# Letting the first three loads of w2 wait only for the last readers of their buffers

## The chip, the cores and the metric

One NeuronCore of a Trainium2 chip. The time is the device time of one execution in microseconds (us). Every run also records the span from first to last instruction and the mean granted TensorE clock (1.0 is full speed). A run is labelled slow because it is over 1.5% above the fastest of its kernel, and is left out of the comparison.

Names in the profiles: PE is the matrix engine and PEld its loads of weights, DVE the vector engine, ACT the scalar engine, and SPq the queue of the SP engine, which issues the transfers (DMA). In this program the matmuls read their operands from SBUF (`arena` in the profiles) and add up their products in banks of PSUM (`ps`).

A ratio is the mean time of one kernel's fast runs over the mean of the other's in the same rounds, so it is not quite the ratio of the medians that are quoted. Ratios carry a 95% interval.

## The reference, cut to what matters

```python
def reference(A_x, A_wqkv, A_wo, B_x, B_w1, B_b1, B_w2, B_b2, gate_w):
    x = A_x                                            # (1, 2048, 512) bf16
    g = sigmoid((x * gate_w).sum(-1, keepdims=True))
    a = local_attention(x, A_wqkv) @ A_wo              # 32 heads, window 8, dilation 2
    h = layernorm(x)                                   # the MLP is called with x as well
    u = gelu(einsum("bsd,sf->bdf", h, w1) + b1)        # w1: 2048 x 1792
    b = (einsum("bdf,fs->bds", u, w2) + b2).transpose(0, 2, 1)   # w2: 1792 x 2048
    return g * a + (1 - g) * b
```

(Condensed.) The end of the kernel computes 16 output tiles of 128 rows. Each is 14 matmuls with w2 (the second product of the MLP) and 4 with wo (the projection of the attention output), accumulated in one PSUM bank. w2 comes in as eight blocks of 256 columns (896 KB); one block serves two output tiles.

## The kernel before

The kernel lists its operations with resource names that they read and write. A small scheduler of its own orders them on each engine, then turns dependences into semaphore waits. A later writer of a name depends on the last writer and on all readers since.

```python
    def add(self, eng, fn, dur, reads=(), writes=(), deps=(), after=(), prio=0, name="", delay=0.0):
        ...
        for d in deps:
            if d is not None:
                op.deps.add(d)          # a wait
        for d in after:
            if d is not None:
                op.order.add(d)         # order of issue only, no wait
        ...
        for w in writes:
            lw = self.last_w.get(w)
            if lw is not None:
                op.deps.add(lw)
            for rd in self.readers.get(w, ()):
                op.deps.add(rd)
            self.readers[w] = []
            self.last_w[w] = op
        ...
    def users(self, names):             # last writers and readers, without becoming a writer
        ...
```

Memory is overlaid. w2 has three block buffers: two in the space of an attention buffer called pb1, one in the space of the wqkv weights.

```python
        W2S = [view("PBUF", BF16, [(256, NFT), (1, 256)], extra=4 * S),
               view("PBUF", BF16, [(256, NFT), (1, 256)], extra=4 * S + NFT * 256),
               view("WQKV", BF16, [(256, NFT), (1, 256)])]
```

The first three loads:

```python
        def ld_w2(j2):
            ds = sch.dsem("w2_%d" % j2)
            al = []
            if j2 < 2:
                al = ["pb1"]
            elif j2 == 2:
                al = ["wqkv%d_%d" % (tn, dt) for tn in range(3) for dt in range(4)]
            return sch.dma("sp", mk_dma(W2S[j2 % 3], w2v[:, :, 256 * j2:256 * j2 + 256]), F * 256 * 2, ds,
                           writes=["w2s%d" % (j2 % 3)] + al, after=d_w1[-1:], name="d_w2_%d" % j2)
        for j2 in range(3):
            ld_w2(j2)
```

Blocks 0 and 1 both "write" pb1, though their bytes do not overlap. So block 1 depends on block 0 having landed.

The same SP queue issues 16 SBUF-to-SBUF copies of the attention weights, `er0r` (4, small) and `er1`, `er2`, `er3` (4 each, 288 KB each). The first four feed the end of the first quarter of a DVE chain (line 776), the others its second, third and fourth quarter. The projection matmuls read its outputs. The consumers at the end:

```python
        for i in range(NST):                       # 16 output tiles
            j2 = i // 2
            bank = YB[i % len(YB)]                 # 7 PSUM banks, so PE may run ahead with w2
            ...
            for half in range(2):                  # line 839 (840 after the change)
                last_main[0] = A("pe", f_ph3(i, bank, half), 1.515, reads=[... "w2s%d" % (j2 % 3)], ...)
            if i % 2 == 1 and j2 + 3 <= 7:
                ld_w2(j2 + 3)
            A("pe", f_wo(i, bank), 0.865, reads=["ot%d" % (i // 4), "wo"], ...)   # line 848 (849)
            ...
```

## Time and profile before

| | before |
|---|---|
| time, median of the first 3 runs (these and a later one: 184.32 to 184.94) | 184.63 us |
| PE busy | 92% of the span |
| PE's longest wait | 9.7 us, for a load of w2 |
| mean granted clock | 0.972 |

The page of before: PE's busy time, then 40 slices of 4.6 us each, with PE's busy share and the granted clock in tenths.

```profile
PE 167.9 (92%) x876; PEld 79.3 (43%) x892; DVE 139.7 (76%) x118; ACT 66.3 (36%) x94; POOL 0.9 (0%) x8
...
PE   7999999999999999999999993059999999999993
...
PEclk9999999999999999999999999756999999999999
```

PE is busy but for one hole in slices 24 to 26, and the clock dips just behind it. The waits of PE in before (us in total, times, longest) name the hole:

```profile
PE ps L839 <- DMA arena<-in_B_w_dram: 9.7, 1, 9.7
```

PE's timeline of before (start, us, engine, line, operation, count, idle time before and its releaser):

```profile
105.03 6.21 PE L839 MATMUL ps<-arena 128*128 128x512 bf16 x28
120.91 16.65 PE L839 MATMUL ps<-arena 128*128 128x512 bf16 x62 [9.67 <-DMA arena<-in_B_w_dram]
```

Two output tiles (28 matmuls, block 0), then nothing until block 1 lands. The SP queue's timeline of before shows why it lands late:

```profile
84.97 5.80 SPq L439 DMA_DIRECT2D arena<-in_B_w_dram  x3
90.81 21.38 SPq L439 DMA_DIRECT2D arena<-arena  x16
112.24 24.20 SPq L439 DMA_DIRECT2D arena<-in_B_w_dram  x4
```

The three loads at 84.97 are the last block of w1, then blocks 0 and 2 of w2. The 16 copies follow, and block 1 goes out only at 112.24. The chain that ended last, in before (start, us, what):

```profile
110.65 1.55 SPq L439
...
112.24 8.62 DMA arena<-in_B_w_dram
...
120.91 6.07 PE ps L839 x14
...
127.03 10.52 PE ps L839 x48
```

The chain runs through the issue of the copies into block 1's load and then PE. The first 14 matmuls take 6.07 us, twice what 14 take elsewhere (3.02).

In this trace the granted clock changed on a grid of 3.413 us: its half-speed stretch is 10.24 us (three times 3.413), its full-speed stretches are 112.64 us (33 times) and 58.03 us (17 times). Stretches laid on that grid are called clock windows here. Columns: from:to, length, then busy time (count) of PE, PEld, DVE, ACT and POOL, then granted clock, DMA share, GB/s.

```profile
109.70:113.11 3.41, 1.54 (x8) 0.49 (x5) 3.41 (x2) 0.00 (x0) 0.00 (x0) 1.00 0.97 184
113.11:116.53 3.42, 0.00 (x0) 0.00 (x0) 3.42 (x3) 0.00 (x0) 0.00 (x0) 1.00 0.79 180
116.53:119.94 3.41, 0.00 (x0) 0.00 (x0) 3.41 (x3) 0.00 (x0) 0.00 (x0) 0.50 0.92 278
119.94:123.36 3.42, 2.45 (x6) 0.89 (x7) 3.35 (x3) 0.00 (x0) 0.00 (x0) 0.50 0.83 218
123.36:126.77 3.41, 3.41 (x9) 1.22 (x8) 3.38 (x2) 0.00 (x0) 0.00 (x0) 0.50 0.00 0
126.77:130.18 3.41, 3.36 (x16) 1.57 (x16) 3.41 (x2) 0.00 (x0) 0.00 (x0) 1.00 0.00 0
```

In this trace the window with PE busy for 45% (1.54 of 3.41) was followed by full clock (1.00), the wholly idle one after it by half clock (0.50).

### The profile page before, as it was taken

What the parts mean: (1) busy time and instruction counts of PE and PEld (TensorE: products, weight loads), DVE (VectorE), ACT (ScalarE), POOL (GpSimd) and SP (SyncE); (2) the same over time, 40 slices, a digit from 0 to 9 for tenths busy, and PEclk for the clock granted to TensorE, in tenths of its full rate; (3) what the DMA queues carried; (4) which work ended last, traced back from release to release, by engine and by line L of the source; (5) the groups of instructions that cost most, each with busy time, mean ns of one, the idle gap of its engine ahead of it and who ended that gap; (6) DMA issues with size and microseconds to landing.
All of it is one profiled execution on the core that took longest, in us unless ns stands there. A gap on an engine that the chain in (4) does not pass through costs nothing.

```text
span 183.0 us, 2127 instructions
## 1 busy us (share of the span) xinstructions
PE 167.9 (92%) x876; PEld 79.3 (43%) x892; DVE 139.7 (76%) x118; ACT 66.3 (36%) x94; POOL 0.9 (0%) x8
## 2 busy tenths in 40 slices
PE   7999999999999999999999993059999999999993
PEld 2855455454444444444444441023444444444441
DVE  0755679999799993689999999999999999800000
ACT  2476668775391115794121110000001231111165
POOL 1000000000000000000000000000000000000000
PEclk9999999999999999999999999756999999999999
DMA  5999799900000626179999899780247356300014
GB/s 184 296 234 235 178 266 314 246 0 5 0 2 5 171 59 188 45 220 243 295 290 214 205 195 185 219 228 0 79 126 228 106 152 193 94 29 31 30 65 135
DMA packets 43101, 27.42 MB, mean 150 GB/s; under 512 B 7892, under 2 KB 42324, under 8 KB 42708
## 3 DMA queue, kind: packets, MB, share of 16 engines
q1 hardware_dynamic: 43092, 27.28, 59.5%
q8 instruction: 7, 0.11, 0.2%
q14 instruction: 2, 0.02, 0.0%
HBM read 18.88 MB, written 2.10 MB: 115 GB/s over the span
## 4 chain that ended last, share of the span: by engine, by line
PE 68%; SPq 11%; DVE 7%; DMA 7%; ACT 4%; issue 1%
PE ps L839 25%; PE ps L586 19%; SPq L439 11%; PE ps L800 9%; PE ps L848 8%; DMA arena<-in_B_w_dram 5%; PE ps L668 4%; DMA arena<-in_A_wqkv_dram 2%; DVE arena L713 2%; DVE arena L776 2%; PE ps L609 2%; DVE arena L761 2%; ACT arena L727 1%; ACT L727 1%; ACT L564 1%
## 5 line engine op out<-in xcount | busy, mean ns | idle before, releaser
L776 DVE TENSOR_TENSOR arena<-arena 128x2048 bf16<-128x2048 bf16 (+2 forms) x32 | 71.5, 2287 | 0.4
L839 PE MATMUL ps<-arena 128*128 128x512 bf16 x220 | 52.8, 395 | 9.9 <-DMA arena<-in_B_w_dram 9.7
L800 PE MATMUL ps<-arena 128*128 128x512 bf16 x218 | 48.5, 379 | 0.3
L839 PEld LDWEIGHTS ps<-arena 128*128 128x128 bf16 x224 | 22.6, 101 | 38.5 <-DMA arena<-in_B_w_dram 10.2
L586 PE MATMUL ps<-arena 128*128 128x512 bf16 x171 | 38.3, 379 | 0.6 <-issue 0.2
L661 DVE TENSOR_TENSOR arena<-arena 128x8192 bf16<-128x8192 bf16 x8 | 35.0, 4421 | 1.2 <-ACT arena L597 1.2
L866 ACT ACTIVATE arena<-ps,arena 128x512 bf16<-128x512 f32 x16 | 12.4, 777 | 62.5 <-PE ps L848 62.0
L800 PEld LDWEIGHTS ps<-arena 128*128 128x128 bf16 x224 | 21.7, 98 | 26.8 <-issue 0.8
L586 PEld LDWEIGHTS ps<-arena 128*128 128x128 bf16 x176 | 19.6, 114 | 18.6 <-ACT arena L597 0.6
L597 ACT ACTIVATE arena<-ps 128x512 bf16<-128x512 f32 x32 | 19.0, 598 | 7.1 <-PE ps L586 6.9
L813 ACT ACTIVATE arena<-ps,arena 128x512 bf16<-128x512 f32 x14 | 9.6, 687 | 30.8 <-PE ps L800 30.7
L848 PE MATMUL ps<-arena 128*128 128x512 bf16 x63 | 15.4, 379 | 0.1
L551 DVE BATCH_NORM_STATS2 arena<-arena 128x6 f32<-128x512 bf16 x16 | 9.9, 680 | 6.6 <-DMA arena<-in_A_x_dram 6.6
L848 PEld LDWEIGHTS ps<-arena 128*128 128x128 bf16 x64 | 6.3, 98 | 7.5
L713 DVE TENSOR_TENSOR arena<-arena 128x256 bf16<-128x256 bf16 (+4 forms) x16 | 7.9, 506 | 2.0 <-ACT arena L727 1.7
L594 ACT ACTIVATE arena<-ps 128x512 bf16<-128x512 f32 x12 | 7.2, 596 | 3.1 <-PE ps L586 3.1
L668 PE MATMUL ps<-arena 128*32 128x512 bf16 x128 | 7.5, 380 | 0.0
L698 ACT ACTIVATE arena<-ps 128x1024 bf16<-128x1024 f32 x4 | 4.0, 1020 | 5.0 <-PE ps L638 3.8
L570 DVE TENSOR_SCALAR arena<-arena 128x512 bf16<-128x512 bf16 x16 | 5.3, 405 | 0.0
L668 PEld LDWEIGHTS ps<-arena 128*32 128x32 bf16 x128 | 3.1, 96 | 4.1 <-issue 0.4
L513 PE MATMUL ps<-arena 128*128 128x512 bf16 x9 | 3.7, 563 | 1.1 <-POOL arena L426 1.1
L609 PE MATMUL ps<-arena 128*128 128x256 bf16 x32 | 3.7, 273 | 0.2 <-DMA arena<-in_A_wqkv_dram 0.2
(50 smaller groups left out, 36.4 us busy)
## 6 DMA issues: line engine op xcount, KB each, us to landing
arena<-in_B_w_dram SPq DMA_DIRECT2D x7, 1024.0 KB, 6.4
arena<-in_B_w_dram SPq DMA_DIRECT2D x8, 896.0 KB, 7.0
arena<-arena SPq DMA_DIRECT2D x12, 288.0 KB, 5.8
arena<-in_A_x_dram SPq DMA_DIRECT2D x4, 512.0 KB, 5.1
out_dram<-arena SPq DMA_DIRECT2D x16, 128.0 KB, 1.7
arena<-in_A_wqkv_dram SPq DMA_DIRECT2D x3, 512.0 KB, 4.5
arena<-arena SPq DMA_DIRECT2D x8, 128.0 KB, 3.0
arena<-in_A_wo_dram SPq DMA_DIRECT2D x1, 512.0 KB, 8.1
```

The lines of the kernel that those rows point to most:

```text
L439: return lambda e: e.dma_start(dst, src)
L551: A("dve", (lambda t_: (lambda e: e.bn_stats(out=ST6[:, t_, :], in_=X[:, t_, :])))(t), 0.7, reads=["x%d" % t], writes=["st6_%d" % t], name ...
L586: ins = e.matmul(ps[:, bank, :], lhsT=lhsT, rhs=XT[:, sb, dt, :], start=(dt == 0), stop=(dt == 3))
L597: return lambda e: e.activation(out=dst, in_=ps[:, bank, :], func=AF.Copy)
L661: return lambda e: e.tensor_tensor(out=PBL[buf], in0=in0, in1=in1, op=ALU.mult)
L668: ins = e.matmul(ps[32 * c:32 * c + 32, 4 + wl, :], lhsT=RP, rhs=PBL[buf][:, wl, c * 512:(c + 1) * 512], start=(dl == 0), stop=(dl == 3), ...
L713: return A("dve", lambda e: e.tensor_tensor(out=o_, in0=a_, in1=b_, op=op_), dur, reads=rd, writes=wr, name=nm)
L776: A("dve", lambda e: e.tensor_tensor(out=o_, in0=a_, in1=b_, op=op_), dur, reads=rd, writes=wr, name=nm)
L800: ins = e.matmul(ps[:, bank, :], lhsT=W1W[:, slot, st, 128 * e_:128 * e_ + 128], rhs=X[:, st, :], start=(st == 0), stop=(st == NST - 1))
L839: ins = e.matmul(ps[:, bank, :], lhsT=W2S[slot][:, ft, 128 * e_:128 * e_ + 128], rhs=UT[:, ft, :], start=(ft == 0), stop=False)
L848: ins = e.matmul(ps[:, bank, :], lhsT=OT[:, t, 128 * i:128 * i + 128], rhs=WO[:, t, :], start=False, stop=(t == 3))
L866: A("act", (lambda e, i=i, bank=bank: e.activation(out=OUTS[:, i, :], in_=ps[:, bank, :], func=AF.Identity, scale=col(OMG, i), bias=col(C2 ...
```

## The change

The intent: the loads should depend only on the last users of the memory that they overwrite, and be issued in the order in which they are read.

```diff
         def ld_w2(j2):
             ds = sch.dsem("w2_%d" % j2)
-            al = []
-            if j2 < 2:
-                al = ["pb1"]
-            elif j2 == 2:
-                al = ["wqkv%d_%d" % (tn, dt) for tn in range(3) for dt in range(4)]
-            return sch.dma("sp", mk_dma(W2S[j2 % 3], w2v[:, :, 256 * j2:256 * j2 + 256]), F * 256 * 2, ds,
-                           writes=["w2s%d" % (j2 % 3)] + al, after=d_w1[-1:], name="d_w2_%d" % j2)
+            al = w2_al[0 if j2 < 2 else 1] if j2 < 3 else ()
+            op = sch.dma("sp", mk_dma(W2S[j2 % 3], w2v[:, :, 256 * j2:256 * j2 + 256]), F * 256 * 2, ds,
+                         writes=["w2s%d" % (j2 % 3)], deps=al, after=(d_w1[-1:] + d_w2[-1:]) if j2 < 3 else (), name="d_w2_%d" % j2)
+            d_w2.append(op)
+            return op
+
+        d_w2 = []
+        w2_al = [sch.users(["pb1"]), sch.users(["wqkv%d_%d" % (tn, dt) for tn in range(3) for dt in range(4)])]
         for j2 in range(3):
             ld_w2(j2)
```

In the scheduled program this swaps blocks 1 and 2 in the SP queue and drops one wait. The other engines' orders stay. The diff also adds an order of issue among the three loads (`after=`).

## The prediction

> **What bounds the kernel now.** The page gives PE 92% busy and 68% of the chain that ended last. The waits by engine show one long PE wait: the matmuls of line 839 (second MLP product, w2) wait 9.7 us for a load of w2. PE's timeline: 28 matmuls of line 839 (output tiles 0 and 1, from the first w2 buffer) end at 111.2 us, then nothing until 120.91. The clock table (windows of 2 us) shows the second cost: granted clock 1.0 until about 116.5, then 0.5 until about 126.8, so the first 14 matmuls after the hole take 6.07 us where every later batch of 14 takes 3.02.
>
> Why that load is late: it is w2 block 1. Blocks 0 and 1 name the same overlaid resource as written, so block 1 waits for block 0's completion. The scheduler therefore places it after block 2 and after the 16 SBUF-to-SBUF copies (issued 90.81 to 112.2 us). It is issued at 112.24 and lands at 120.86 (8.62 us in the chain). Blocks 0 and 2, issued before the copies, land at about 94.5 and 97.6; block 2 is not read before tile 4. By 112 the wait itself is long satisfied: what costs is the place in the SP queue.
>
> **What the change does.** The instruction orders of PE, DVE, ACT and POOL stay. On SP, blocks 1 and 2 swap places and one wait (on block 0) goes. No work is added or removed. So block 1 should land near 97.6 us, and block 2 should be issued near 112.2 and land near 120.9.
>
> **Critical path.** PE then runs tiles 2 and 3 straight on: 28 x 0.216 = 6.05 us, 111.2 to 117.2. It waits for block 2 from 117.2 to 120.9, about 3.7 us instead of 9.7. Gain for certain: 6.0 us. Second term, the clock. [...] the slow stretch is 10.24 us, three times 3.41, and starts 5.3 us after PE went idle. [...] I expect the clock mostly to stay at 1.0, which saves the other 3.0 us (6.07 less 3.02). Sum: 9.0 us with the clock kept, 6.0 if it falls. I give the kept clock about three in four.
>
> What could take it back: tile 6 needs block 3, which lands at 123.7 now and is wanted at 127. Block 4 can be issued at 117.3 instead of 130, and is wanted after 132. The DVE chain (line 776) ends at 159.5 and feeds the last group of output-projection matmuls of line 848, which start at 174.0 now and would start at 165. Each keeps several us of slack, so the gain should last to the end.
>
> **Prediction.** 175.9 us (184.63 less 9.0, plus part of the chance of a cold clock), 8 in 10 between 175.0 and 179.0. Chances: faster by over 2% 0.96, within 2% 0.03, slower 0.01.
>
> **What would show it right.** One PE wait of 3 to 4 us for a w2 load in place of 9.7; 56 matmuls of line 839 before it; a clock of 1.0 through it; the matmuls after it at 3.0 us per 14; the 16 copies and the DVE chain where they were; the last PE group near 165.
>
> **What would make it wrong.** The clock falling to 0.5 at a 3.7 us hole (result about 178.6). Block 2, now behind the copies, landing later than 121. Block 1 not landed by 111. Block 4's earlier issue slowing blocks 2 or 3. PE running into the DVE chain.

The reasons given for the second term are cut where marked, since no trace of this case shows them. 6.0 us for the hole and 3.0 us for the clock (6.07 less 3.02) make 9.0, and 6.0 if the clock falls.

## The result, and the profile after

| | before | after |
|---|---|---|
| time, median of 4 runs (range) | 184.49 (184.32 to 184.94) | 178.54 (177.09 to 178.89) |
| ratio | | 0.9659 (0.96 to 0.9718) |
| PE's wait for a w2 load | 9.7 | 3.8 |
| mean granted clock of the 4 runs | 0.972 in the profiled run | 0.990, 0.989, 0.990, 0.990 |

The page of after (slices of 4.4 us; PE is now 95% busy):

```profile
PE   7999999999999999999999999974999999999993
...
PEclk9999999999999999999999999997899999999999
```

The hole is narrower, but the clock still dips. The waits of PE in after:

```profile
PE ps L840 <- DMA arena<-in_B_w_dram: 3.8, 1, 3.8
```

PE's timeline and, in the second fence, the SP queue's timeline of after:

```profile
105.61 12.25 PE L840 MATMUL ps<-arena 128*128 128x512 bf16 x56
121.64 9.36 PE L840 MATMUL ps<-arena 128*128 128x512 bf16 x35 [3.79 <-DMA arena<-in_B_w_dram]
```

```profile
85.54 6.08 SPq L439 DMA_DIRECT2D arena<-in_B_w_dram  x3
91.66 21.46 SPq L439 DMA_DIRECT2D arena<-arena  x16
113.16 7.83 SPq L439 DMA_DIRECT2D arena<-in_B_w_dram  x3
```

Four tiles (56 matmuls) now run before the hole instead of two. The copies stand where they stood, and the load behind them is now block 2. The trace's completion events put block 1 at 98.5 us, block 2 at 121.6. The chain that ended last, in after:

```profile
113.16 8.43 DMA arena<-in_B_w_dram
...
121.64 9.36 PE ps L840 x35
131.00 0.86 PE ps L849 x4
```

The 35 matmuls behind the hole take 9.36 us; at full clock 35 take 7.73 (an experiment's trace below). The clock windows of after, laid on this trace's own grid, with the columns as before:

```profile
118.17:121.58 3.41, 0.00 (x0) 0.00 (x0) 3.39 (x3) 0.00 (x0) 0.00 (x0) 1.00 1.02 299
121.58:124.99 3.41, 3.35 (x8) 1.19 (x9) 3.32 (x3) 0.00 (x0) 0.00 (x0) 0.50 1.20 291
124.99:128.40 3.41, 3.41 (x17) 1.57 (x16) 3.41 (x1) 0.00 (x0) 0.00 (x0) 1.00 0.43 110
```

The spans differ by 6.60 us (183.0 and 176.4). The sum from the two traces: the hole, 3.79 less 9.67, gives -5.88. From the first w2 matmul to the first projection matmul, without the hole, before takes 137.56 - 105.03 - 9.67 = 22.86 and after 131.00 - 105.61 - 3.79 = 21.60: -1.26, the clock. The first w2 matmul starts 0.58 later in after, in a part that the change does not touch (PE waits 0.5 there for a load of x): +0.58. From the first projection matmul to the end, 45.44 and 45.40: -0.04.

So the hole gave what it should. The clock, expected to give 3.0, gave 1.3 in this pair of traces.

### The profile page after: what moved, and what is told of

Same layout as the page of the kernel before. It is cut to its first block, busy times and chain, and to the rows that moved or that the text cites. A ratio compares the mean times of both kernels' runs of the same rounds, so it can differ in the third digit from the quotient of the medians.

```text
span 176.4 us, 2143 instructions
## 1 busy us (share of the span) xinstructions
PE 168.1 (95%) x892; PEld 79.4 (45%) x892; DVE 139.7 (79%) x118; ACT 66.3 (38%) x94; POOL 0.9 (0%) x8
## 4 chain that ended last, share of the span: by engine, by line
PE 58%; SPq 17%; DMA 11%; DVE 8%; ACT 4%; issue 1%
PE ps L840 22%; PE ps L586 14%; SPq L439 12%; PE ps L800 10%; PE ps L849 8%; DMA arena<-in_B_w_dram 5%; SPq L460 4%; PE ps L668 4%; DMA arena<-in_A_x_dram 4%; DMA arena<-in_A_wqkv_dram 3%; DVE arena L713 3%; DVE arena L776 2%; DVE arena L761 2%; ACT arena L727 1%; ACT L727 1%
## 5 line engine op out<-in xcount | busy, mean ns | idle before, releaser
L542 DVE COPY arena<-ps 128x512 bf16<-128x512 bf16 x2 | 0.8, 425 | 4.0 <-PE ps L525 3.9
```

## The experiments

Every experiment gave a correct result. Ratios are to the kernel before, in the same rounds (its medians in the experiments: 184.6, 184.4, 184.69). "Runs with a dip" are those with a mean clock of 0.99 or less (0.989 and below included); the others have 0.997 or more.

| run | edit | median us | ratio (95% interval) | hole in its trace | runs with a dip |
|---|---|---|---|---|---|
| after (first result) | none | 178.54 | 0.9659 (0.96 to 0.9718) | 3.79 | 4 of 4 |
| e1_old_place_no_wait | blocks in the old places, no wait | 184.46 | 1.001 (0.9946 to 1.0074) | 9.93 | 4 of 4 |
| e2_new_place_wait | new places, wait kept | 179.97 | 0.9757 (0.9702 to 0.9812) | 5.95 | 4 of 4 |
| e3_after_fill16 | after, hole filled | 176.26 | 0.9561 (0.9515 to 0.9607) | 0.53 | 0 of 6 |
| e4_before_fill43 | before, hole filled | 182.18 | 0.9879 (0.9833 to 0.9926) | 0.26 | 0 of 6 |
| e5_after_fill3 | after, 3 fillers | 177.99 | 0.9647 (0.9608 to 0.9686) | 3.42 | 5 of 6 |
| e8_after_fill5 | after, 5 fillers | 177.29 | 0.9641 (0.9596 to 0.9686) | 2.74 | 5 of 6 |
| e5b_after_fill8 | after, 8 fillers | 175.52 | 0.9525 (0.949 to 0.9559) | 1.83 | 0 of 5, and the slow run |
| after_again | none | 178.18 | 0.9671 (0.9632 to 0.971) | 3.80 | 6 of 6 |
| e6_three_ahead | three blocks ahead of the copies | 173.48 | 0.9409 (0.9373 to 0.9446) | 0.86 | 0 of 4 |
| e7_third_mid | block 2 between the copies | 172.23 | 0.9347 (0.9302 to 0.9392) | none | 0 of 4 |

Four kernels move a load in the SP queue after scheduling and before waits are planned, so that dependences are kept:

```diff
         total_est = sch.schedule()
+        def mv(name, behind):
+            sp = sch.order["sp"]
+            op, prev = [[o for o in sp if o.name == n_][0] for n_ in (name, behind)]
+            sp.remove(op)
+            sp.insert(sp.index(prev) + 1, op)
+            op.start = prev.start + 1e-6
         sch.plan_waits()
```

### Is it the wait or the place in the queue? (e1, e2)

The theory was that the wait had long been satisfied when block 1's turn came, and that its effect was to make the scheduler put block 1 behind the copies. The rival was that the wait itself cost the time.

e1, on the changed kernel:

```diff
+        mv("d_w2_2", "d_w2_0")
+        mv("d_w2_1", "d_er3_3")
```

> The changed kernel with blocks 1 and 2 of w2 put back in their old places in the SP queue (block 1 behind the 16 copies), but still without the wait on block 0. Theory (the place in the queue is everything, the wait itself had long been satisfied): the same as the kernel before, 184.5 us within 0.5 %, with a hole of 9.7 us before the matmuls of the third output tile and about 10 us of clock at 0.5. Rival (the removed wait is what gains): 178.5 us, as the changed kernel.

Measured: 184.46 us, ratio 1.001. PE's timeline of e1:

```profile
121.17 15.65 PE L840 MATMUL ps<-arena 128*128 128x512 bf16 x62 [9.93 <-DMA arena<-in_B_w_dram]
```

The wait is gone, the 9.9 us hole is back, and so is the time. The wait by itself was worth nothing where it stood.

e2, the converse, on the changed kernel:

```diff
         for j2 in range(3):
             ld_w2(j2)
+        d_w2[1].deps.add(d_w2[0])
...
+        mv("d_w2_1", "d_w2_0")
```

> The changed kernel with the same order of the SP queue, but block 1 again waits for block 0 to land. Theory: block 0 lands at about 95.5 us, so the SP queue stands from about 89.5 to 95.5 and the copies behind it start near 96 instead of 91.7; they then catch up partly[...]. Block 2 lands 2 to 4 us later than 121.6, the hole grows from 3.8 to 6 to 8 us, the DVE chain starts its second quarter later; time 180.5 to 182.5. Rival (the wait costs nothing at all, wherever it stands): 178.5.

Measured: 179.97 us, a small miss: less loss than the 180.5 to 182.5 expected. The SP queue's timeline of e2:

```profile
84.82 9.90 SPq L439 DMA_DIRECT2D arena<-in_B_w_dram  x3
94.76 19.32 SPq L439 DMA_DIRECT2D arena<-arena  x16
```

The wait holds the queue (9.90 us for three loads instead of 6.08). The copies behind it catch up part of that (19.32 us instead of 21.46), all of it at the first copy (0.85 us instead of 3.10); the other fifteen take 18.43 us here and 18.32 in after. Block 1's load took the queue 2.95 us to issue in after, behind loads that had not landed, and 0.37 us in e2, where the queue had first waited for block 0 to land. That the outstanding transfers cause this was not tested. The hole grows to 5.95 us and the DVE chain waits 1.3 us for a copy. So with the old wait the new place still gives most of the gain (ratio 0.9757 against 0.9659). Dropping the wait is needed only so that the queue does not stand in the new place.

### What does the clock cost? (e3, e4)

Matmuls of no use, ones times ones into a PSUM bank that nobody reads any more, keep PE busy in the hole. On the changed kernel (e4: on the kernel before, `i == 2` and 43):

```diff
         for i in range(NST):
...
+            if i == 4:
+                last_main[0] = A("pe", f_warm_on(16, 3), 0.01, reads=["ones"], writes=["bank3"],
+                                 after=[last_main[0]], name="fill", prio=0)
             for half in range(2):
```

> The changed kernel with 16 matmuls of no use (3.46 us at full clock, into a PSUM bank that nobody reads) in the hole of 3.8 us before the fifth output tile. Theory (the matmuls behind the hole ran at half clock for one window because the hole was idle): the clock stays at 1.0 through the hole, the 35 matmuls behind it take 7.6 us instead of 9.36, and the time falls by about 1.8 us, to 176.7. Rival (the slow 35 matmuls come from something else, such as data or transfers landing): the clock still falls or the matmuls stay at 9.4 us; 178.5.

> The kernel before with 43 matmuls of no use (9.29 us at full clock) in its hole of 9.7 us. Theory: the load still lands near 120.9, the clock stays at 1.0, the 14 matmuls behind the hole take 3.0 us instead of 6.07, and the time falls by about 3.0 us, to 181.5. That is the clock's share of the hole in the kernel before. Rival: no change, 184.5.

PE's timeline behind the fillers, in e3 and then in e4:

```profile
121.10 7.73 PE L840 MATMUL ps<-arena 128*128 128x512 bf16 x34 [0.53 <-DMA arena<-in_B_w_dram]
```

```profile
120.67 13.54 PE L839 MATMUL ps<-arena 128*128 128x512 bf16 x61 [0.26 <-DMA arena<-in_B_w_dram]
```

(A matmul or two is missing from such counts in a trace.) Both expectations held, e4's with 182.18 us where 181.5 was expected. The load still lands when it did; the matmuls behind it run at full speed: 7.73 us instead of 9.36 after, 13.54 instead of 16.65 before.

The four kernels (hole as it was or shortened, clock dipping or kept) form a square. With the clock kept, shortening the hole is worth (0.9879 - 0.9561) x 184.6 = 5.9 us. The prediction had 6.0. The dip costs (1 - 0.9879) x 184.6 = 2.2 us before (interval 1.4 to 3.1; the trace says 16.65 - 13.54 = 3.1). After, it costs (0.9659 - 0.9561) x 184.6 = 1.8 us, across two calls (the trace says 9.36 - 7.73 = 1.6). So of the dip's cost the change saves 1.5 us by the traces (3.1 less 1.6) and 0.4 us by the ratios (2.2 less 1.8), whose intervals of 0.8 us and more either way are too wide to tell the two apart. It shortens the dip, but does not remove it.

### Why does the clock fall at a hole of 3.8 us? (e5, e5b, after_again, e8)

The trace of before (full clock after the window of 45%, half clock after the idle one) allows two theories. Theory A, on which the prediction counted: the clock falls only after a wholly idle window. A 3.8 us hole holds one only for (3.79 - 3.41) / 3.41 = 11% of the grid's positions, an estimate from the trace's hole and grid. Yet all four runs of after dipped, and the one traced had just that position. Theory B: a window that is mostly idle is enough. The experiments shrink the hole with fewer fillers (3, 8 or 5 in place of 16 in the diff above).

> The changed kernel with 3 matmuls of no use (0.65 us) at the start of its hole, which so shrinks from 3.8 to about 3.15 us: less than one clock window of 3.41 us, so no window can be wholly idle. Theory A (the clock falls only after a window that is wholly idle, and the changed kernel's four runs with clock 0.99 just met that phase): the mean clock is 0.998 or more in all runs and the time is about 176.7 us. Theory B (a window that is mostly idle is enough): the mean clock is 0.99 in most runs, the time 177 to 178.5.

> The same with 8 matmuls (1.73 us), which leaves a hole of about 2.1 us, at most 60 % of a window. Theory A and a theory B with its threshold above 60 % idle: clock 0.998 or more in all runs, 176.7 us. Theory B with a lower threshold: 0.99 in some runs.

> The changed kernel again, unaltered, for more runs and a second trace. Theory B, now with the threshold between 55 and 67 % idle that the traces so far allow: with a hole of 3.8 us nearly every phase of the window gives a drop, so the mean clock is 0.99 in at least five of six runs, and the time is 178.3 us within 1 us. Theory A (only a wholly idle window): 0.998 or more in most runs and about 176.7 us.

> The changed kernel with 5 matmuls of no use (1.08 us) at the start of the hole, which leaves 2.7 to 2.9 us, always shorter than a window. Theory B: a drop in roughly half to nine tenths of the runs, which shows as a mean clock of 0.99, and a bimodal time, near 178 with the drop and near 176.3 without; in the trace the window that ends with a drop is at least 55 % idle. Theory A: never a drop, 176.3 us.

Clock windows of after_again, then of e5, e8 and the end of e7 (a kernel of the next section), each on its trace's own grid and with the columns as before (PE busy follows the length, the clock is third from the end).

```profile
116.64:120.05 3.41, 0.54 (x3) 0.04 (x1) 3.41 (x3) 0.00 (x0) 0.00 (x0) 1.00 0.92 277
120.05:123.47 3.42, 2.49 (x6) 0.89 (x7) 3.32 (x4) 0.00 (x0) 0.00 (x0) 0.50 1.19 296
123.47:126.88 3.41, 3.41 (x9) 1.21 (x8) 3.41 (x1) 0.00 (x0) 0.00 (x0) 0.50 0.67 168
```

```profile
119.73:123.15 3.42, 1.13 (x6) 0.54 (x7) 3.35 (x4) 0.00 (x0) 0.00 (x0) 1.00 1.12 299
123.15:126.56 3.41, 3.41 (x10) 1.18 (x9) 3.38 (x2) 0.00 (x0) 0.00 (x0) 0.50 1.07 264
```

```profile
117.04:120.45 3.41, 1.47 (x7) 0.49 (x5) 3.41 (x3) 0.00 (x0) 0.00 (x0) 1.00 0.96 282
120.45:123.86 3.41, 2.60 (x13) 1.18 (x14) 3.31 (x4) 0.00 (x0) 0.00 (x0) 1.00 1.18 296
123.86:127.28 3.42, 3.42 (x17) 1.55 (x16) 3.42 (x1) 0.00 (x0) 0.00 (x0) 1.00 0.62 156
```

```profile
162.77:166.18 3.41, 3.41 (x18) 1.51 (x17) 0.00 (x0) 3.07 (x5) 0.00 (x0) 1.00 0.34 115
166.18:169.59 3.41, 1.19 (x6) 0.34 (x4) 0.00 (x0) 1.83 (x3) 0.00 (x0) 1.00 0.45 154
169.59:170.28 0.69, 0.00 (x0) 0.00 (x0) 0.00 (x0) 0.00 (x0) 0.00 (x0) 0.50 0.00 0
```

Windows that were 16% busy (0.54 of 3.41), 33% (1.13 of 3.42) and, at the end of e7, 35% (1.19 of 3.41) were each followed by half clock. One that was 43% busy (1.47 of 3.41) was not, nor the one of 45% in the kernel before. So theory A falls: these windows of up to 35% busy were followed by half clock, those of 43% and 45% were not. An average over two windows does not fit: e8 kept the clock after 43% and 76%, e7 lost it after 100% and 35%. The grid of e8 is that of its first rise and last fall of the clock, 170.67 us apart, 50 times 3.413.

The counts agree: all ten runs of the changed kernel dipped. So did 5 of 6 runs with 3 fillers, where the hole was always expected to be shorter than a window; in the traced one it was 3.42 us, since block 2 landed a little later. With 5 fillers, 5 of 6 dipped; the traced run, with a hole of 2.74 us, is the one that did not. With 8 fillers none of the five fast runs did. The sixth has a mean clock of 0.99, but it is the run labelled slow: it lies 2.6 us above the others' median, more than one half-speed window costs (9.36 - 7.73 = 1.6), so nothing is read from it. In e8 the undipped run took 176.19 us, the others 177.2 to 178.74.

In after_again the dip lasted two windows: the clock did not rise after the first, which was 73% busy (2.49 of 3.42), but after the second, which was wholly busy. That trace's 35 matmuls took 10.62 us instead of 9.36, so its dip cost 2.9 us (10.62 - 7.73), nearly as much as the 3.1 of before. The mean clock of each run tells how often this happens: by an estimate (1 - 0.5 x 3.41 / 176) one half-speed window gives 0.990; two give 0.981 and three the 0.972 of before. So nine of the ten runs of the changed kernel had one such window, and one had two.

### Is the rest of the hole block 2 behind the copies? (e6, e7)

```diff
+        mv("d_w2_2", "d_w2_1")        # e6: all three ahead of the copies
```
```diff
+        mv("d_w2_2", "d_er1_3")       # e7: behind the copies for the second quarter, ahead of the others
```

> All three first loads of w2 ahead of the 16 copies. Theory (the rest of the hole is block 2 standing behind the copies): no hole at all, clock at 1.0, so 178.5 less 3.8 less 1.8: about 172.9 us. The copies start about 3 us later and the second quarter of the DVE chain waits 2 to 3 us for them, which the last projection matmuls just tolerate (third quarter's output wanted near 164, ready near 162.5). Rival (the transfers collide and the hole moves to the DVE chain or to block 3): 175 or more.

> Block 2 of w2 issued after the copies for the second quarter of the DVE chain and before those for the third and fourth, which have slack. Theory: block 2 lands near 110 us, no hole before the fifth tile, DVE chain where it was; block 3 goes out near 116 and lands at 122 to 125 where tile 6 wants it at 123, so a hole of 0 to 1.5 us may stay; clock 1.0; 173 to 174.5 us. Rival as before: 175 or more.

PE's timeline of e6 behind its first 84 w2 matmuls, then the line of its DVE timeline that holds the second to fourth quarter:

```profile
124.85 1.68 PE L840 MATMUL ps<-arena 128*128 128x512 bf16 x7 [0.86 <-DMA arena<-in_B_w_dram]
```

```profile
108.55 53.94 DVE L776 TENSOR_TENSOR arena<-arena 128x8192 bf16<-128x8192 bf16 x24 [2.36 <-DMA arena<-arena]
```

e6 ran at 173.48 us. (Its trace holds no record of the clock; its 84 matmuls in 18.29 us, 0.218 us each, ran at full speed.) The DVE chain waits 2.36 us for the later copies, without effect on the end, as expected. The expected absence of a hole was a small miss: 0.9 us remains, now for block 3, which also stands behind the copies.

PE's timeline of e7, then its SP queue:

```profile
105.04 19.80 PE L840 MATMUL ps<-arena 128*128 128x512 bf16 x91
```

```profile
90.83 9.35 SPq L439 DMA_DIRECT2D arena<-arena  x8
100.22 1.49 SPq L439 DMA_DIRECT2D arena<-in_B_w_dram  x1
101.75 12.18 SPq L439 DMA_DIRECT2D arena<-arena  x8
```

All 91 matmuls run without a hole in 19.80 us, and the DVE chain starts its second quarter on time. e7 took 172.23 us, a little below the expected 173 to 174.5: block 3 landed at 122.8 us, just in time, so the small hole allowed for did not appear. It beats both kernels, by 6.5% against before. Its chain is PE almost from end to end, so in this trace nothing in the SP queue bounds it any more.

## Why the prediction was right or wrong

The measured 178.54 us lies inside the stated range of 175.0 to 179.0, near its upper end and 2.6 us above the stated 175.9. The range was wide enough for both outcomes of the clock (175.6 with it kept, 178.6 with it lost), so lying inside it says nothing for that step.

- **"what costs is the place in the SP queue"**: right. e1 removes the wait alone and gains nothing (1.001); e2 keeps the wait in the new place and gains most (0.9757).
- **Block 1 near 97.6, block 2 landing near 120.9**: right, 98.5 and 121.6 us. Block 2, issued behind all the copies, lands 4.3 us after the last of them (117.3).
- **"Gain for certain: 6.0 us"** from the hole: right. The trace shows 5.88; with the clock kept in both kernels the runs show 5.9.
- **"I expect the clock mostly to stay at 1.0, which saves the other 3.0 us"**, with the kept clock at "three in four": this is the step that failed. The clock fell in all ten runs of the changed kernel. The prediction counted on a drop only after a wholly idle window; the traces show one also after windows that were 16%, 33% and 35% busy. The term of 3.0 measured 1.3 us in the first pair of traces (0.4 by the ratios, within wide intervals), since the dip is shorter (one or two windows instead of three) rather than gone.
- **Slack at the end**: right. From the first projection matmul to the end the traces agree to 0.04 us; PE waits for nothing but the w2 load there.
- **"The clock falling to 0.5 at a 3.7 us hole (result about 178.6)"**: named as what would make it wrong, and what happened, at 178.54.

The prediction took the measured phase of one trace and assumed, which the trace did not show, that only a wholly idle window counts. The trace of before could not contradict it: there the window of 45% kept the clock and the next was wholly idle.

## What to carry to other kernels

When a false dependence is removed, ask what it did to the order of a queue before asking what the wait cost: here the satisfied wait cost nothing, and the place behind 16 copies cost everything. A hole in PE's work also cost clock behind it here: all ten runs of the changed kernel dipped (3.8 us in both traces), and five of six with 5 fillers (2.74 us in the one traced, which kept the clock), but none of the five fast runs with 8 (1.83 us in the trace). By an estimate from the window of 43%, a hole under 1.9 us (3.41 less 1.47) is the safer figure for this kernel. So close such a hole wholly or fill it, and do not count on the chance that it misses a window. And where a load is moved out of a queue's tail, look at which load is there now: moving block 2 between the copies took away a further 6 us.
